# Two query chunks interleaved, a negation moved to VectorE, twelve more tiles on VectorE, three more warm products

## The chip, the cores and the metric

One Trainium2 chip, one core. The time is device microseconds of one execution of the whole program; lower is better. Engine names in the profile: PE is TensorE (PEld its weight loads), ACT is ScalarE, DVE is VectorE, POOL is GpSimd, SP is SyncE, whose queue issues most DMAs.

## The reference

Two attention blocks read the same `x` (2048 tokens, 512 wide, 32 heads of 16) and are mixed by a gate per token:

```python
g = sigmoid((x * gate_w).sum(-1, keepdims=True))
# a: softmax attention
scores = einsum("bhqd,bhkd->bhqk", q, k) * Dh ** -0.5
a = einsum("bhqk,bhkd->bhqd", softmax(scores), v) @ A_wo
# b: linear attention with softmax features
pq, pk = q @ w_phi[h], k @ w_phi[h]
phi_q = concat([softmax(pq), softmax(-pq)])       # phi_k likewise from pk
kv, z = einsum("bhsf,bhsd->bhfd", phi_k, v), phi_k.sum(s)
b = ((phi_q @ kv) / (phi_q @ z + 1e-6)) @ B_wo
out = g * a + (1 - g) * b
```

Branch A has 32 x 2048 x 2048 exponentials, which is by far the largest piece of elementwise work. Branch B has the features, their sums, and a small matrix per head.

## The kernel before

**Branch A.** The queries are cut into 4 chunks (`qc`) of 512, the heads into 4 pairs of groups (`cp`, 128 columns, each with two sides). A *group* is one chunk, one `cp` and one side: four heads of it lie in the four strips of 32 rows of the PE array. There are 32 groups. Each group runs over 16 key tiles of 128 tokens; a key tile of a group is a *row* of the schedule, numbered `p` from 0 to 511, and consists of 4 *units* of 128 keys x 512 queries, one per head. So a group is 64 units, and the kernel has 2048. Each unit is a score product (`_scores`, L1015, into PSUM), an exponential, and a value product (`_values`, L1122) that adds into the group's accumulator, one PSUM bank. Groups follow each other in the order chunk, `cp`, side: first all of chunk 0, then all of chunk 1, and so on.

**Two engines take the exponentials.** Most units go through ScalarE, two at a time (`_exp`, L1063, 128x1024 from a ring of four PSUM banks into `ET`). The rest, `NUMS[g]` of the 64 in group `g`, go to VectorE in batches of four (`_vector_batch`): VectorE writes the bits of an approximate power of two (L922, one 128x512 instruction per unit, from PSUM), and two more instructions per batch (L947, 2048 and 4096 elements) make three shifted copies. All four copies go through value products, two of them with the scaled values `V2`, so a unit on VectorE costs four value products where a unit on ScalarE costs one. `NUMS` adds up to 488 units (x488 at L922).

**Feeding it.** `_proj_k` (evacuated at L770), `_proj_v` (L819) and `_proj_q` (L783, then a mask on GpSimd at L788) make the keys, values and queries of a `cp` shortly before its rows. `_proj_q0`/`_proj_k0` do the first 512 tokens in two halves of 256, since `x` arrives in pieces by transposing DMAs; nine products on constant data (`_warm`, L689) run on PE before that. After a group, `_norm` transposes the accumulator (L1143), and after both sides it scales by reciprocal row sums and the gate, and sends the result back through DMAs on the SP queue into `onTA`.

**Branch B** is work for the gaps of the same engines. `_b_pair` handles two token tiles: two products with their evacuations (L1281), the negated copy (`b_neg`, L1299, GpSimd), maxima (L1302, L1304), a subtraction (L1307), one exponential on ScalarE (L1310), sums and reciprocals, the last mostly on GpSimd (L1314 to L1373), and a product (L1357). All of this is a chain on one buffer. Keys come first (8 pairs, due from row 30 on, every 23 rows, with `_b_v`, L1258, and `_b_kv`, L1400), then queries (8 pairs, due from row 214 on, every 30.5 rows, followed by `_b_den` and `_b_num`, L1451 to L1475). `_gate` computes the gate and copies it (`ghB`, L862, four small copies named `gate_b`). `_out` adds both output projections in PSUM and writes the tile out (L1599); in the last chunk alternate tiles go over ScalarE (L1596).

**The order is planned when the program is built.** `Plan.order` simulates the five engines with a table of costs and puts every operation into a fixed queue per engine; at run time each engine goes through its queue and waits on semaphores. Operations carry a due row (`prio`), an earliest row (`rel`) and a row from which they go ahead of everything (`urgent`). Names in `PORT` may not overlap GpSimd's work in the plan. `SEEDS` shifts the due rows by pseudo-random amounts, so that another set of numbers gives another order throughout. Where PE would idle, the plan puts in products with zeros (L1129, "fills"), which keep the array at work; `PADK` is the number of the first ScalarE score group that may be padded so in the start. Four PSUM banks are the ring of ScalarE, the other four are shared by accumulators, VectorE's scores and all projections.

Of the kernel before, what the change touches and what calls it, by code (L numbers as in the profile page):

```python
# [10 lines left out]
P = 128  # L11
# [54 lines left out]
class Plan:  # L66
# [70 lines left out]
        self.ops.append(o)  # L137
        return o

    SEEDS = (6713, 8236, 795, 8928, 4203, 3987, 4548, 4431, 3369, 6855, 1992, 9096, 3816, 673, 8476, 4153, 2488, 5053, 9892, 380, 9864, 6961, 8928, 7398, 8610, 6258, 6732, 8778, 7190, 2318, 6568, 0, 527, 0)  # L140

    def shift(self):
        count = {}
# [30 lines left out]
    SAME = 100  # L174
    OPEN = 2
    HURRY, FREE = 20, 30
    PORT = ("v_step", "b_neg", "b_max", "b_sub", "b_sum", "b_total", "b_mul", "n_mul", "n_den", "kvbd")
    HOLDING = ("kproj", "qproj", "bv", "pq", "vproj", "outa", "outb", "wtr", "xtr")

    def rank(self, o):  # L180
# [227 lines left out]
class _Kernel:  # L408
# [8 lines left out]
    KEEP = 15  # L417
    URGENT, AHEAD, SOON, REST = 4, -(1 << 30), 4, 6
    QDUE, KDUE, VDUE = 20, 17, 14
    P_Q, P_MUL, P_NEG = 1, 1, 1  # L420
    P_REC, P_SUM = 0, 4
    P_BACK, RATIO, BV = 1, 1, 8
    DEN, KV2, P_MAX = 1, 0, 0
    REND = 5
    P_M, P_BMUL, CHUNKS = 0, 0, 2
    GDUE = 26
    VMIN = 8
    FAST = 3
    VSOON = -2
    PADK = 8  # L430
    LAST, FIRST_OUT, NEXT_OUT, DEP_OUT = 0, 8, 0, 2
    ALONE, EARLY = 12, 10
    PVP = 10
# [1 line left out]
    def __init__(self, nc, A_x, A_wqkv, A_wo, B_wqkv, B_w_phi, B_wo, gate_w, out):  # L435
        self.nc = nc
        self.x2d = A_x.flatten_outer_dims()
        self.A_wqkv, self.A_wo = A_wqkv, A_wo
        self.B_wqkv, self.B_w_phi, self.B_wo = B_wqkv, B_w_phi, B_wo
        self.gate_w, self.out2d = gate_w, out.flatten_outer_dims()  # L440
        self.S = self.x2d.shape[0]
        self.NT = self.S // TOK
        self.NQC = self.S // QCH
        self.NPACK = self.NQC * 8 * self.NT
        self.plan = Plan()

    def build(self):
        with ExitStack() as ctx:
# [233 lines left out]
        job.bank = bank  # L682
        return job, (job if bank is None else None)

    def _warm(self, n, after):

        def run(e):
            for _ in range(n):
                ins = e.matmul(self.ps[:, 4, :], self.warm[:, 0:P], self.warm[:], start=True, stop=True)  # L689
            return ins  # L690
        self.plan.op("PE", run, 0.427 * n, reads=[self.b_warm], deps=[after], name="warm", prio=-99)

    COLS = 0

# [44 lines left out]
    def _proj_q0(self, half, bank):  # L739

        lo, op, ends = 256 * half, self.plan.op, []
        job, pool = self._job(bank)
        m = None
        for c in range(4):
            m = op("PE", lambda e, c=c: e.matmul(self._bank(job)[:, 0:256], self.WA[:, 0, c, 0:P],
                                                 self.xT[:, c, lo:lo + 256], start=(c == 0), stop=(c == 3)),
                   self.c_pe(256), reads=[self.b_x0[half], self.b_WA[0][0]], deps=[m], name="qproj", prio=half - 2.2,
                   acquire=None if c else pool)
            m.urgent = half - 99
        for side in range(2):  # L750
            dst, by = self.qT[:, side, lo:lo + 256], self.mask[:, side:side + 1]
            if half or side:
                o = op("DVE", lambda e, dst=dst, by=by: e.tensor_scalar(dst, self._bank(job)[:, 0:256], by, None,
                                                                        op0=ALU.mult), self.c_dve(256) + 0.06,
                       deps=[m] + ends, reads=[self.b_mask], name="q0_ev", prio=side - 2, release=pool if side else None)
            else:
                o = op("ACT", lambda e, dst=dst, by=by: e.activation(dst, self._bank(job)[:, 0:256], ACT.Copy, scale=by),
                       self.c_act(256) + 0.1, deps=[m], reads=[self.b_mask], name="q0_ev", prio=-2)
            self.b_qT[side].writers.append(o)
            if side == 0:  # L760
                self.b_q0[half].writers.append(o)
            ends.append(o)
        self.early.setdefault(bank, []).extend(ends)

    def _proj_k(self, cp, j):
        due = 32 * cp + 3 * j - self.KDUE if cp else 4 * j - 2.0
        self._proj(lambda c: self.WA[:, 1, c, P * cp:P * cp + P],
                   lambda c: self.xT[:, c, QCH * j:QCH * j + QCH],
                   [self.b_xT[j], self.b_WA[1][cp > 0]],
                   [lambda e, b: e.tensor_copy(self.kT[:, cp, QCH * j:QCH * j + QCH], b)],  # L770
                   self.c_dve(512), due, due - (24 if cp else 99), "kproj", [self.b_kT[cp][j]],
                   urgent=32 * cp + 4 * j - self.SOON)

    def _proj_q(self, qc, cp):
        n = qc * 4 + cp
        due = 32 * n - self.QDUE
        s0 = 2 * (n % (self.NQS // 2))

        lhs, rhs = lambda c: self.WA[:, 0, c, P * cp:P * cp + P], lambda c: self.xT[:, c, QCH * qc:QCH * qc + QCH]
        reads = [self.b_xT[qc], self.b_WA[0][cp > 0], self.b_mask]  # L780
        if self.P_Q:
            tmp, b_tmp = self.qtmp[:, n % 2, :], self.b_qtmp[n % 2]
            o = self._proj(lhs, rhs, reads, [lambda e, b: e.tensor_copy(tmp, b)], self.c_dve(512), due, 32 * n - 30, "qproj",  # L783
                           [b_tmp], urgent=32 * n - self.SOON)
            o.deps += [r for r in b_tmp.readers if r not in o.deps]
            b_tmp.readers = []
            for side in range(2):
                x = self.plan.op("POOL", lambda e, side=side: e.tensor_scalar(  # L788
                    self.qT[:, s0 + side, :], tmp, self.mask[:, side:side + 1], 0.0, op0=ALU.mult, op1=ALU.add), 0.7,
                    reads=[b_tmp, self.b_mask], writes=[self.b_qT[s0 + side]], name="qmask", prio=due + 1)  # L790
                x.urgent = o.urgent
            return
        self._proj(lhs, rhs, reads,
                   [lambda e, b: e.tensor_tensor(self.qT[:, s0:s0 + 2, :], b[:, None, :].to_broadcast([P, 2, QCH]),
                                                 self.mask[:, :, None].to_broadcast([P, 2, QCH]), ALU.mult)],
                   self.c_dve(1024), due, 32 * n - 30, "qproj", [self.b_qT[s0]], urgent=32 * n - self.SOON)
        self.b_qT[s0 + 1] = self.b_qT[s0]

    def _proj_v(self, pr, t0):

        op, NT = self.plan.op, self.NT
        job = Job()
        due = 64 * pr + t0 - (self.VDUE if pr else 0.5)
        mm = None
        for tt in range(2):
            def run(e, tt=tt):
                out = self._bank(job).rearrange("p (c t x) -> p c t x", c=2, t=2)[:, :, tt, :]
                for c in range(4):
# [2 lines left out]
                return ins  # L811
            mm = op("PE", run, 4 * self.c_pe(256), reads=[self.b_xT[t0 // 4], self.b_WA[2][pr]], deps=[mm], name="vproj",
                    prio=due, rel=due - 24 if pr else 0 if t0 < 4 else -99, acquire=None if tt else job)
            mm.urgent = 64 * pr + t0 - self.VSOON
        lo, n = t0 * self.VCP, 2 * self.VCP
        both = lambda v: v[:, 2 * pr * NT * self.VCP:(2 * pr + 2) * NT * self.VCP].rearrange(
            "p (c x) -> p c x", c=2)[:, :, lo:lo + n]
# [47 lines left out]
                prio=100))  # L865
        self.b_gB.writers = done

    NUMS = (6, 10, 12, 14, 14, 15, 13, 16, 13, 20, 17, 13, 16, 13, 19, 21, 10, 18, 12, 16, 19, 13, 17, 16, 15, 20, 12, 19, 17, 16, 23, 13)

    def _plan_vector(self):  # L870

        NT, away = self.NT, []
# [8 lines left out]
            self.hooks.setdefault(max(0, int(due) - 4), []).append(  # L881
                lambda k=k, units=units, due=due: self._vector_batch(k, units, due))
        for n in range(1, 4 * self.NQC):
            self.hooks.setdefault(max(0, 32 * n - 30), []).insert(0, lambda n=n: self._proj_q(*divmod(n, 4)))
        self.away = set(away)

    def _value_bufs(self, bufs, p, spill):

        kt, cp = p % self.NT, p // (2 * self.NT) % 4
        at = cp * self.NT + kt  # L890
        found = list(bufs[cp][kt // 2].writers)
        if spill and at + 1 < 4 * self.NT:
# [3 lines left out]
    def _vector_batch(self, number, units, due):  # L896
# [46 lines left out]
        for k in range(4):  # L943
# [9 lines left out]
            for g in sorted({u // (4 * NT) for u in units}):  # L953
# [3 lines left out]

                def run(e, g=g, src=src, ot=ot, v=v, tile=tile, place=place):
                    for j, u in src:
                        ins = self._values(e, ot, g % 8, u // 4 % NT, {u % 4: tile[:, place(j), :].bitcast(BF16)}, v)  # L960
                    return ins
                x = op("PE", run, 0.23, reads=[buf], deps=list(found.values()), name="pvx", prio=units[0] / 4 - 2,
                       kind="col", array=0.0533 * len(src), strips=[u % 4 for _, u in src])
# [5 lines left out]
    def _attention(self):  # L969
# [24 lines left out]
        while a < len(self.mine):  # L994
# [4 lines left out]
            done = self.mine[a] if a < len(self.mine) else NU  # L999
            while len(self.pvs) < done // 4:  # L1000
                self._pv(len(self.pvs))
                if len(self.pvs) % (8 * NT) == 0:
                    self._out(len(self.pvs) // (8 * NT) - 1)

    def _unit(self, u):

        p, i = divmod(u, 4)
        g, kt = divmod(p, self.NT)
        qc, g8 = divmod(g, 8)
        s = 2 * ((qc * 4 + g8 // 2) % (self.NQS // 2)) + g8 % 2  # L1010
        return p, i, kt, g8 // 2, s

    def _scores(self, e, u, out, cols=slice(0, QCH)):
# [56 lines left out]
    def _pv(self, p):  # L1070
# [13 lines left out]
        def run(e):  # L1084
            for _ in range(o.filled):
                self._fill(e, ot)
            return self._values(e, ot, g % 8, kt, src, self.V)
        o = self.plan.op("PE", run, 0.23, reads=[self.b_zero], deps=deps, name=f"pv{p}", prio=p + self.PVP, kind="col",
                         acquire=None if kt else ot, array=0.0533 * len(src), strips=list(src))
        plan = self.plan  # L1090
# [40 lines left out]
        return ins  # L1131

    def _norm_a(self, g, last):
        qc, g8 = divmod(g, 8)
        return self._norm(qc, lambda: self._bank(self.ot[g]), g8 % 2, last, self.onTA[:, qc % 3, g8 // 2, :],
                          self.b_onTA[qc % 3][g8 // 2], 16 * g + 17.0, self.ot[g], g >= self.NPACK // self.NT - 2)

# [430 lines left out]
    def _out(self, qc):  # L1568
        op, NT, NQC = self.plan.op, self.NT, self.NQC
        for tt in range(4):  # L1570
            t = 4 * qc + tt
            final = qc == NQC - 1
            due = max(128 * (qc + 1) + 8 + 4 * tt, self._num_due(t) + 8)
            job, first = self.outs[t]
            b_onTA = self.b_onTA[qc % 3]
            if final:
# [70 lines left out]
```

## Time and profile before

| | |
|---|---|
| three runs | 767.77 us median, 766.18 to 769.58 |
| the profiled execution | 767.62 us; span on the core 765.6 us |
| ScalarE busy | 749.1 us, 98% of the span |
| TensorE busy (modelled ends) | 739.6 us, 97% |
| VectorE busy | 711.6 us, 93% |
| GpSimd busy | 207.5 us, 27% |
| granted TensorE clock | 0.997 of full in the mean |

The profile's page gives busy time per engine, the span in 40 slices, the chain of waits that ended last, and groups of equal instructions with their busy time, the mean duration of one and the idle time before them. Instructions on one engine overlap a little: a mean duration is longer than busy time over count, and the distance of two starts is the better price. The span runs from the first to the last instruction; what lies around it is the 2.0 us between 765.6 and 767.62.

### The profile page before, as it was taken

What the parts mean: (1) busy time and instruction counts of PE and PEld (TensorE: products, weight loads), DVE (VectorE), ACT (ScalarE), POOL (GpSimd) and SP (SyncE); (2) the same over time, 40 slices, a digit from 0 to 9 for tenths busy, and PEclk for the clock granted to TensorE, in tenths of its full rate; (3) what the DMA queues carried; (4) which work ended last, traced back from release to release, by engine and by line L of the source; (5) the groups of instructions that cost most, each with busy time, mean ns of one, the idle gap of its engine ahead of it and who ended that gap; (6) DMA issues with size and microseconds to landing.
All of it is one profiled execution on the core that took longest, in us unless ns stands there. A gap on an engine that the chain in (4) does not pass through costs nothing.

```text
span 765.6 us, 17042 instructions
## 1 busy us (share of the span) xinstructions
PE 739.6 (97%) x7149; PEld 219.6 (29%) x7220; DVE 711.6 (93%) x1110; ACT 749.1 (98%) x804; POOL 207.5 (27%) x301
## 2 busy tenths in 40 slices
PE   8999999999999999999999999999999999999998
PEld 3322233222222222222332322232222222222222
DVE  4778997899999999999999999999999999999995
ACT  6999999999999999999999999999999999999996
POOL 2210255315053260405145023422314140250000
PEclk9999999999999999999999999999999999999999
DMA  9501001000000000010121202211111121011000
GB/s 232 127 2 28 3 14 15 1 2 8 9 3 14 1 3 14 1 15 2 15 29 28 53 11 51 45 27 30 32 26 28 29 47 24 15 30 27 5 12 28
DMA packets 89180, 20.78 MB, mean 27 GB/s; under 512 B 83472, under 2 KB 88592, under 8 KB 89104
## 3 DMA queue, kind: packets, MB, share of 16 engines
q1 hardware_dynamic: 87232, 18.92, 13.4%
q8 instruction: 56, 0.92, 0.5%
q10 hardware_dynamic: 1872, 0.79, 0.4%
q14 instruction: 20, 0.16, 0.1%
HBM read 4.21 MB, written 2.10 MB: 8 GB/s over the span
## 4 chain that ended last, share of the span: by engine, by line
ACT 76%; PE 15%; DVE 9%; issue 1%
ACT ET L1063 73%; PE ps L1015 5%; PE ps L1122 5%; PE ps L698 3%; ACT bq L1310 3%; DVE vs L922 3%; DVE vs L947 2%; PE ps L1129 1%; PE ps L689 1%; DVE onB L1475 1%; DVE T L1143 0%; DVE bq L1307 0%; DVE btree L1304 0%; DVE ghB L862 0%; DVE qtmp L783 0%
## 5 line engine op out<-in xcount | busy, mean ns | idle before, releaser
L1063 ACT ACTIVATE ET<-ps 128x1024 bf16<-128x1024 f32 (+1 forms) x782 | 720.4, 1154 | 3.7 <-PE ps L1015 3.6
L922 DVE TENSOR_SCALAR vs<-ps 128x512 uint16<-128x512 f32 x488 | 313.7, 679 | 20.7 <-PE ps L1015 19.7
L1015 PE MATMUL ps<-qT,kT 32*128 32x512 bf16 (+1 forms) x2052 | 312.4, 385 | 13.1 <-ACT ET L1063 8.0
L947 DVE TENSOR_SCALAR vs<-vs 128x2048 uint16<-128x2048 uint16 (+1 forms) x244 | 235.4, 977 | 1.9 <-PE ps L1122 0.5
L1122 PE MATMUL ps<-vs,V 128*32 128x512 bf16 x1952 | 216.4, 384 | 1.4 <-DVE vs L947 1.4
L1122 PE MATMUL ps<-ET,V 128*32 128x512 bf16 x1560 | 194.5, 387 | 0.1
L1015 PEld LDWEIGHTS ps<-qT,kT 32*128 32x128 bf16 x2052 | 78.0, 91 | 309.3 <-ACT ET L1063 293.2
L1314 POOL TENSOR_TENSOR btree<-btree 128x512 f16<-128x512 f16 (+1 forms) x32 | 33.4, 1044 | 188.8 <-DVE btree L1312 188.0
L1122 PEld LDWEIGHTS ps<-ET,V 128*32 128x32 bf16 x1560 | 48.9, 94 | 84.1 <-issue 75.8
L1129 PE MATMUL ps<-kT,zero 128*32 128x512 bf16 x628 | 63.4, 385 | 0.0
L1122 PEld LDWEIGHTS ps<-vs,V 128*32 128x32 bf16 x1952 | 49.8, 95 | 45.9 <-issue 27.5
L1299 POOL TENSOR_SCALAR bq<-bq 128x1024 bf16<-128x1024 bf16 x16 | 21.5, 1341 | 150.6 <-DVE bq L1281 119.5
L698 PE MATMUL ps<-WB,xT 128*128 128x512 bf16 x160 | 49.6, 383 | 2.8 <-issue 2.1
L1160 POOL TENSOR_TENSOR T<-T,rinv 128x512 bf16<-128x512 f32 x15 | 18.2, 1210 | 83.4 <-DVE rinv L1158 83.2
L698 PE MATMUL ps<-xT,WA 128*128 128x512 bf16 x101 | 33.2, 392 | 1.9 <-issue 1.6
L788 POOL TENSOR_SCALAR qT<-qtmp,mask 128x512 bf16<-128x512 bf16 x30 | 25.8, 866 | 28.8 <-DVE qtmp L783 28.5
L1143 DVE STREAM_TRANSPOSE T<-ps 128x512 f32<-128x512 f32 x32 | 22.6, 707 | 11.2 <-PE ps L1122 11.1
L1310 ACT ACTIVATE bq<-bq 128x2048 bf16<-128x2048 bf16 x16 | 32.1, 2007 | 0.2
L1281 DVE CAST bq<-ps 128x512 bf16<-128x512 f32 x32 | 21.7, 680 | 0.3 <-PE ps L698 0.2
L826 POOL TENSOR_SCALAR V<-V 128x544 bf16<-128x544 bf16 x16 | 12.6, 788 | 33.4 <-DVE V L819 33.2
L698 PEld LDWEIGHTS ps<-WB,xT 128*128 128x128 bf16 x192 | 13.3, 97 | 25.3 <-issue 20.5
L1129 PEld LDWEIGHTS ps<-kT,zero 128*32 128x32 bf16 x628 | 14.7, 94 | 19.7 <-issue 18.8
(88 smaller groups left out, 405.3 us busy)
## 6 DMA issues: line engine op xcount, KB each, us to landing
T<-T SPq DMA_DIRECT2D x240, 8.0 KB, 1.8
WB<-in_B_wqkv_dram SPq DMA_DIRECT2D x1, 1536.0 KB, 7.9
out_dram<-WB SPq DMA_DIRECT2D x12, 128.0 KB, 1.7
WA<-in_A_wqkv_dram SPq DMA_DIRECT2D x2, 384.0 KB, 5.4
WoB<-in_B_wo_dram SPq DMA_DIRECT2D x1, 512.0 KB, 3.8
WoA<-in_A_wo_dram SPq DMA_DIRECT2D x1, 512.0 KB, 4.8
WA<-in_A_wqkv_dram ACTq DMA_DIRECT2D x2, 128.0 KB, 3.1
WA<-in_A_wqkv_dram ACTq DMA_DIRECT2D x1, 256.0 KB, 4.6
```

Of the source, the lines that this page charges most:

```text
L698: return e.matmul(out, lhs, rhs, start=start, stop=stop)
L788: x = self.plan.op("POOL", lambda e, side=side: e.tensor_scalar(self.qT[:, s0 + side, :], tmp, self.mask[:, side:side + 1], 0.0, op0=ALU.m ...
L922: bits = lambda e, to, src: e.tensor_scalar(to, src, SCALE * LOG2E * 128.0, float(ORIGIN), op0=ALU.mult, op1=ALU.add)
L947: o = op("DVE", lambda e, k=k, src=src, dst=dst: e.tensor_scalar(dst, src, float(STEPS[k - 1]), None, op0=ALU.add), 0.16 + k * n * QCH * 0 ...
L1015: return e.matmul(out[:, cols], self.kT[32 * i:32 * i + 32, cp, kt * TOK:(kt + 1) * TOK], self.qT[32 * i:32 * i + 32, s, cols], start=True ...
L1063: o = plan.op("ACT", lambda e: e.activation(self.ET[:, a % NS:a % NS + n, cols], self.ps[:, a % NR:a % NR + n, cols], ACT.Exp, scale=SCALE ...
L1122: ins = e.matmul(self._bank(ot)[32 * i:32 * i + 32, :], v[:, v0:v0 + 32], tile, start=(kt == 0), stop=(kt == self.NT - 1), tile_position=( ...
L1129: ins = e.matmul(self._bank(ot)[32 * i:32 * i + 32, :], self.zero[:], self.kT[:, 0, 0:QCH], start=False, stop=False, tile_position=(0, 32 ...
L1143: t1 = op("DVE", lambda e: e.transpose(T1[:, side].rearrange("p b s -> p (b s)"), src()), 0.735, deps=last, writes=[b_T1[side]], name="n_t ...
L1281: [lambda e, b, k=k: e.tensor_copy(bq[:, k].rearrange("p (g s v) -> p g s v", g=8, s=2)[:, :, 0, :], b.rearrange("p (g v) -> p g v", g=8))],
L1310: op("ACT", lambda e: e.activation(flat, flat, ACT.Exp), 1.789, reads=[b], writes=[b], name="b_exp", prio=due + 1)
L1314: + [("b_sum", two(128 * n), lambda e, n=n: e.tensor_tensor(half[:, :, 0:n], half[:, :, 0:n], half[:, :, n:2 * n], ALU.add), (n <= self.P_ ...
```

## The change

1. **Order of the groups.** With `PAIRQ = 1`, `self.pairs` lists chunk 0 and chunk 1 alternately for each `cp`: (0, cp 0), (1, cp 0), (0, cp 1), (1, cp 1) and so on to row 256; chunks 2 and 3 follow as before. `use[cp]` is the first row of a `cp`, now 0, 64, 128, 192 in place of 0, 32, 64, 96. The due rows of `_proj_k`, `_proj_q` and `_proj_v` follow it; for the second half of the values `use` is 128 plus the tile, but row 95 for the first two tiles. Chunk 0 is complete at row 224 in place of 128 (`done`), which is when its output may be due.
2. **Warm products.** Three more products on constant data, into bank 1, after the first half of the first query projection (`WARM = 3`).
3. **`P_NEG = 0`**: the 16 `b_neg` go from GpSimd to VectorE.
4. **`NUMS`**: 500 units on VectorE in place of 488. By eight groups: 111, 127, 127, 135 in place of 100, 132, 121, 135.
5. **Plan**: new `SEEDS`, `gate_b` and `gwb` added to `PORT`, `PADK` 2 in place of 8.

```diff
-    SEEDS = (6713, 8236, 795, 8928, 4203, 3987, 4548, 4431, 3369, 6855, 1992, 9096, 3816, 673, 8476, 4153, 2488, 5053, 9892, 380, 9864, 6961, 8928, 7398, 8610, 6258, 6732, 8778, 7190, 2318, 6568, 0, 527, 0)
+    SEEDS = (5206, 4574, 4516, 849, 7476, 2999, 2928, 1228, 1442, 3304, 7242, 2072, 255, 3792, 7272, 0, 9567, 6248, 9008, 9950, 2895, 6157, 2030, 1780, 7230, 8440, 1271, 7931, 6690, 9122, 5090, 0, 4360, 0)
...
-    PORT = ("v_step", "b_neg", "b_max", "b_sub", "b_sum", "b_total", "b_mul", "n_mul", "n_den", "kvbd")
+    PORT = ("v_step", "b_neg", "b_max", "b_sub", "b_sum", "b_total", "b_mul", "n_mul", "n_den", "kvbd", "gate_b", "gwb")
...
-    P_Q, P_MUL, P_NEG = 1, 1, 1
+    P_Q, P_MUL, P_NEG = 1, 1, 0
...
+    PAIRQ = 1
...
-    PADK = 8
+    PADK = 2
...
+        pairs = [(qc, cp) for cp in range(4) for qc in range(2)] if self.PAIRQ else [(qc, cp) for qc in range(2) for cp in range(4)]
+        self.pairs = pairs + [(qc, cp) for qc in range(2, self.NQC) for cp in range(4)]
+        self.seq = [(qc, 2 * cp + side) for qc, cp in self.pairs for side in range(2)]
+        self.use = [32 * next(n for n, x in enumerate(self.pairs) if x[1] == cp) for cp in range(4)]
+        self.done = [32 * max(n + 1 for n, x in enumerate(self.pairs) if x[0] == qc) for qc in range(self.NQC)]
...
+        if self.WARM and not half:
+            self.early.setdefault(1, []).append(self._warm(self.WARM, m, bank=1, cost=0.215, prio=-2.15))
...
-        due = 32 * cp + 3 * j - self.KDUE if cp else 4 * j - 2.0
+        due = self.use[cp] + 3 * j - self.KDUE if cp else 4 * j - 2.0
...
-        due = 64 * pr + t0 - (self.VDUE if pr else 0.5)
+        use = self.use[2 * pr] + t0
+        if pr and not t0:
+            use = min(use, self.use[1] + 31)
+        due = use - (self.VDUE if pr else 0.5)
...
-    NUMS = (6, 10, 12, 14, 14, 15, 13, 16, 13, 20, 17, 13, 16, 13, 19, 21, 10, 18, 12, 16, 19, 13, 17, 16, 15, 20, 12, 19, 17, 16, 23, 13)
+    NUMS = (6, 10, 16, 14, 14, 16, 16, 19, 13, 19, 17, 12, 17, 11, 19, 19, 14, 20, 12, 16, 19, 13, 17, 16, 15, 20, 12, 20, 17, 16, 22, 13)
...
-        kt, cp = p % self.NT, p // (2 * self.NT) % 4
+        kt, cp = p % self.NT, self.pairs[p // (2 * self.NT)][1]
...
-        qc, g8 = divmod(g, 8)
-        s = 2 * ((qc * 4 + g8 // 2) % (self.NQS // 2)) + g8 % 2
+        g8 = self.seq[g][1]
+        s = 2 * (g // 2 % (self.NQS // 2)) + g8 % 2
...
-            due = max(128 * (qc + 1) + 8 + 4 * tt, self._num_due(t) + 8)
+            due = max(self.done[qc] + 8 + 4 * tt, self._num_due(t) + 8)
```

More of the change, by code (lines that the diff above doesn't have):

```diff
@@ L683, in _job, with _warm @@
         return job, (job if bank is None else None)
-    def _warm(self, n, after):
+    def _warm(self, n, after, bank=4, cost=0.427, prio=-99):
         def run(e):
             for _ in range(n):
-                ins = e.matmul(self.ps[:, 4, :], self.warm[:, 0:P], self.warm[:], start=True, stop=True)
+                ins = e.matmul(self.ps[:, bank, :], self.warm[:, 0:P], self.warm[:], start=True, stop=True)
             return ins
-        self.plan.op("PE", run, 0.427 * n, reads=[self.b_warm], deps=[after], name="warm", prio=-99)
+        return self.plan.op("PE", run, cost * n, reads=[self.b_warm], deps=[after], name="warm", prio=prio)
+    WARM = 3
     COLS = 0
@@ L771, in _proj_k, with _proj_q @@
                    self.c_dve(512), due, due - (24 if cp else 99), "kproj", [self.b_kT[cp][j]],
-                   urgent=32 * cp + 4 * j - self.SOON)
-    def _proj_q(self, qc, cp):
-        n = qc * 4 + cp
+                   urgent=self.use[cp] + 4 * j - self.SOON)
+    def _proj_q(self, n):
+        qc, cp = self.pairs[n]
         due = 32 * n - self.QDUE
@@ L813, in _proj_v @@
                     prio=due, rel=due - 24 if pr else 0 if t0 < 4 else -99, acquire=None if tt else job)
-            mm.urgent = 64 * pr + t0 - self.VSOON
+            mm.urgent = use - self.VSOON
         lo, n = t0 * self.VCP, 2 * self.VCP
@@ L883, in _plan_vector @@
         for n in range(1, 4 * self.NQC):
-            self.hooks.setdefault(max(0, 32 * n - 30), []).insert(0, lambda n=n: self._proj_q(*divmod(n, 4)))
+            self.hooks.setdefault(max(0, 32 * n - 30), []).insert(0, lambda n=n: self._proj_q(n))
         self.away = set(away)
     def _value_bufs(self, bufs, p, spill):
-        kt, cp = p % self.NT, p // (2 * self.NT) % 4
+        kt, cp = p % self.NT, self.pairs[p // (2 * self.NT)][1]
         at = cp * self.NT + kt
@@ L959, in run @@
                     for j, u in src:
-                        ins = self._values(e, ot, g % 8, u // 4 % NT, {u % 4: tile[:, place(j), :].bitcast(BF16)}, v)
+                        ins = self._values(e, ot, self.seq[g][1], u // 4 % NT, {u % 4: tile[:, place(j), :].bitcast(BF16)}, v)
                     return ins
@@ L1001, in _attention @@
                 self._pv(len(self.pvs))
-                if len(self.pvs) % (8 * NT) == 0:
-                    self._out(len(self.pvs) // (8 * NT) - 1)
+                if len(self.pvs) in self.done:
+                    self._out(self.done.index(len(self.pvs)))
     def _unit(self, u):
@@ L1086, in run @@
                 self._fill(e, ot)
-            return self._values(e, ot, g % 8, kt, src, self.V)
+            return self._values(e, ot, self.seq[g][1], kt, src, self.V)
         o = self.plan.op("PE", run, 0.23, reads=[self.b_zero], deps=deps, name=f"pv{p}", prio=p + self.PVP, kind="col",
@@ L1133, in _norm_a @@
     def _norm_a(self, g, last):
-        qc, g8 = divmod(g, 8)
+        qc, g8 = self.seq[g]
         return self._norm(qc, lambda: self._bank(self.ot[g]), g8 % 2, last, self.onTA[:, qc % 3, g8 // 2, :],
```

## The prediction

> **What bounds the kernel now.** I read the page first, for the engines and the chain of waits, then the groups by shape, then busy time by stretches.
>
> ```profile
> span 765.6 us, 17042 instructions
> ...
> PE 739.6 (97%) x7149; PEld 219.6 (29%) x7220; DVE 711.6 (93%) x1110; ACT 749.1 (98%) x804; POOL 207.5 (27%) x301
> ...
> DVE  4778997899999999999999999999999999999995
> ACT  6999999999999999999999999999999999999996
> ...
> ACT 76%; PE 15%; DVE 9%; issue 1%
> ```
> ```profile
> L1063 ACT ACTIVATE ET<-ps 128x1024 bf16<-128x1024 f32 x778 | 718.3, 1157 | 3.3 <-PE ps L1015 3.2
> ...
> L1299 POOL TENSOR_SCALAR bq<-bq 128x1024 bf16<-128x1024 bf16 x16 | 21.5, 1341 | 150.6 <-DVE bq L1281 119.5 <-DVE VB L1258 26.4 <-DVE bq L1357 4.6
> ...
> L1302 DVE TENSOR_TENSOR btree<-bq 128x1024 bf16<-128x1024 bf16 x16 | 10.8, 676 | 1.3 <-POOL bq L1299 1.3
> ```
>
> ScalarE carries 76% of the chain, and its 778 full exponentials waited only 3.3 us in all. Outside the start and the tail it is never free. One exponential of two tiles costs 718.3 / 778 = 0.923 us of its time; the 1157 ns include the overlap with the next. VectorE looks free by its average (93%), but the row of slices says where: in the first eight. The next view gives this in microseconds.
>
> ```profile
> core 0: us, PE busy (x) PEld busy (x) DVE busy (x) ACT busy (x) POOL busy (x), PEclk, DMA share, GB/s
> 0.00:20.00 20.00, 17.75 (x94) 6.64 (x96) 9.67 (x19) 12.64 (x16) 5.62 (x17) 0.91 1.00 237
> 20.00:160.00 140.00, 136.40 (x1168) 43.32 (x1180) 117.80 (x181) 138.61 (x151) 35.74 (x51) 1.00 0.12 24
> 160.00:750.00 590.00, 573.28 (x5799) 165.68 (x5852) 577.08 (x901) 589.05 (x629) 166.12 (x233) 1.00 0.12 21
> ```
> ```profile
> 200.00:600.00 400.00, 389.04 (x3883) 113.11 (x3917) 392.33 (x616) 399.15 (x425) 126.32 (x181) 1.00 0.12 21
> 500.00:600.00 100.00, 97.12 (x999) 27.84 (x1004) 98.76 (x156) 99.83 (x108) 27.05 (x36) 1.00 0.14 26
> 160.00:205.00 45.00, 43.53 (x424) 12.82 (x432) 44.61 (x73) 45.00 (x49) 13.79 (x18) 1.00 0.05 7
> ```
>
> VectorE idles 22.2 us between 20 and 160 us (16%), but only 12.9 us in the 590 us after (2.2%). Two engines are full from 160 us on. What counts is whether work can move from ScalarE into VectorE's early gap.
>
> **The change, part by part.**
>
> *Twelve more tiles on VectorE.* ScalarE loses 12 tiles, six exponentials: 6 x 0.923 = **-5.5 us** on the path. VectorE's price is read from distances of starts:
>
> ```profile
> 98.35 1.21 DVE L947 TENSOR_SCALAR vs<-vs 128x4096 uint16<-128x4096 uint16 x1
> 99.48 1.87 DVE L922 TENSOR_SCALAR vs<-ps 128x512 uint16<-128x512 f32 x3
> ...
> 104.00 0.68 DVE L1281 CAST bq<-ps 128x512 bf16<-128x512 f32 x1
> 104.60 0.68 DVE L947 TENSOR_SCALAR vs<-vs 128x2048 uint16<-128x2048 uint16 x1
> 105.20 0.68 DVE L922 TENSOR_SCALAR vs<-ps 128x512 uint16<-128x512 f32 x1
> ```
>
> The 4096 step takes 1.13 us, the 2048 step and a 128x512 piece 0.60 each. A tile is 0.60 plus a quarter of 1.73, that is 1.03 us; twelve are 12.4 us. Eleven of them land in the first eight groups (111 for 100), where the gap is; groups 16 and 17 get six more, groups 8 to 15 give five up. On TensorE each tile has three more value products:
>
> ```profile
> L1122 PE MATMUL ps<-vs,V 128*32 128x512 bf16 x1952 | 216.4, 384 | 1.4 <-DVE vs L947 1.4
> L1122 PE MATMUL ps<-ET,V 128*32 128x512 bf16 x1560 | 194.5, 387 | 0.1
> L1129 PE MATMUL ps<-kT,zero 128*32 128x512 bf16 x628 | 63.4, 385 | 0.0
> ```
>
> That is 48 x 0.111 - 12 x 0.125 = 3.8 us, and the 63.4 us of zero products that fill PE's holes cover it. If the holes lie elsewhere, 3.8 us is the cost.
>
> *The negation.* POOL loses 21.5 us that is off the path; VectorE's maxima waited 1.3 us in all for it. VectorE gains 16 two-byte operations of 1024 elements. Nearest row: L947, the same instruction, 0.60 us for 2048 and 1.13 for 4096, so 0.53 per 2048 and 0.34 for 1024: 5.4 us in all, the value I take. The other end is the pace of a 128x512 copy, 0.60 for 512 elements, with 0.53 more for the other 512: 1.13 each, 18.1 us.
>
> *VectorE's balance.* Between 20 and 750 us it works 117.80 + 577.08 = 694.9 us; now 694.9 + 12.4 + 5.4 = 712.7. ScalarE would need 730 - 5.5 - 1.4 (the stall below) = 723.1. That leaves 10.4 us, 1.4%, for VectorE's idle time. The best 100 us of the trace have 1.24% (cost 0), the 400 us from 200 to 600 have 1.92% (712.7 / 0.9808 = 726.7, cost 3.6), the whole from 160 to 750 has 2.19% (728.7, cost 5.6). Part of that idle time is only pacing by ScalarE and can close; I take the middle of the first two, **+1.8 us**, and keep 0 to 5.6.
>
> *Interleaving.* It removes no work; projections of keys for the second `cp` on move back by 32, 64 and 96 rows, and most of the second half of the values from about row 50-64 to 116-130. It should remove this stall:
>
> ```profile
> 89.92 2.01 DVE L862 COPY ghB<-gh 32x16 f32<-32x16 f32 x4
> ...
> 91.95 0.69 DVE L770 CAST kT<-ps 128x512 bf16<-128x512 f32 x1
> ...
> 92.70 0.38 PE L1015 MATMUL ps<-qT,kT 32*128 32x512 bf16 x1 [1.28 <-DVE kT L770]
> ...
> 94.20 1.94 ACT L1063 ACTIVATE ET<-ps 128x1024 bf16<-128x1024 f32 x2 [1.39 <-PE ps L1015]
> ```
>
> VectorE reaches the evacuation of the keys only after four copies of the gate that took 2.01 us beside GpSimd's work; a score product behind it in PE's queue waits for the bank, and ScalarE idles 1.39 us. With the keys of the third `cp` due 64 rows later, and the copies planned apart from GpSimd, I count **-1.4 us**; the other end is 0, with another crowd there. Chunk 0's output is held back to row 224, which costs nothing: its first evacuation came only when branch B delivered, at 410 us:
>
> ```profile
> L1599 DVE CAST WB<-ps x12: 672/680/692, 410.1 to 636.5; 128x512 bf16<-128x512 f32 x12
> ...
> L819 DVE CAST V<-ps x16: 680/693/695, 15.1 to 140.2; 128x512 bf16<-128x512 f32 x16
> L770 DVE CAST kT<-ps x15: 672/680/694, 13.6 to 174.8; 128x512 bf16<-128x512 f32 x15
> ```
>
> The same normalisations, DMAs of SP's queue, masks on POOL and query projections remain, in another order; none is on the chain, so their move is counted at nothing. If a head pair's return through SP were late, only an output would wait, and outputs have the rows to 750 us.
>
> *Start: warm products and `PADK`.*
>
> ```profile
> 8.22 3.17 ACT L1063 ACTIVATE ET<-ps 128x512 bf16<-128x512 f32 x5 [0.47 <-PE ps L1015]
> 11.94 2.10 ACT L1063 ACTIVATE ET<-ps 128x1024 bf16<-128x1024 f32 x2 [0.55 <-PE ps L1015]
> 14.54 3.84 ACT L1063 ACTIVATE ET<-ps 128x1024 bf16<-128x1024 f32 x4 [0.50 <-PE ps L1015]
> ```
> ```profile
> 7.02:10.43 3.41, 2.76 (x21) 1.30 (x21) 2.00 (x4) 2.69 (x6) 0.00 (x0) 1.00 1.11 235
> 10.43:13.85 3.42, 3.42 (x13) 0.89 (x12) 1.46 (x4) 2.81 (x3) 0.00 (x0) 0.50 1.08 223
> ...
> 7.08 0.33 PEld L745 LDWEIGHTS ps<-xT,WA 128*128 128x128 bf16 x4 [0.38 <-DMA xT<-in_A_x_dram]
> ...
> L689 PE MATMUL ps<-warm 128*128 128x512 bf16 x9 | 4.0, 631 | 1.5 <-DVE warm L620 1.5
> ```
>
> The first exponential starts at 8.22. After a stretch in which PE was busy 2.76 of 3.41 us the granted clock was 0.50 for 3.4 us, and ScalarE waited 0.55 + 0.50 around it: at most -1.05 to gain. Three products at the pace of the nine (4.0 / 9 = 0.45 each) put 1.34 us ahead of the second half of `x`, of which 0.38 was a wait for the DMA anyway: at most +0.96 to lose. With the clock of 1.00 granted from 7.02 on they may take half of that, and the loss is 0.3. Half the gain and that loss give **-0.3 us** (rounded).
> The Trainium skill, "TensorE: Matmul & The Clock Gate", section "What's actually happening", ties the half clock to an idle window of about 3.4 us. By that rule a stretch with 2.76 us busy would not cost the clock, more products would gain nothing, and the sum would be 0.6 us higher; this trace, with 0.50 right after such a stretch, does not agree.
>
> *Sum:* -5.5 + 1.8 - 1.4 - 0.3 = -5.4 us. The profiled execution took 767.6 us for a span of 765.6, and lies 0.15 under the median; so 762.2, and I say **762 us**.
>
> **The rivals.**
>
> *VectorE becomes the bound.* For it: from 160 us on it idles only 2.2%, and groups 16 and 17 with their six new tiles lie where there is no room. Against: 22.2 us of early gap, and branch B's chains are free to move. With the three gains (5.5 + 1.4 + 0.3 = 7.2) and 2.19% idle: 767.6 - 7.2 + 5.6 = 766.0 us, no change. Should the negation cost 1.13 each, the work is 725.4, 734.5 us at 1.24% idle, 11.4 above 723.1: 772.
>
> *The postponed projections crowd rows 96 to 128* (the slower case). That is 160 to 205 us, where VectorE was busy 44.61 of 45. Added there: up to seven value evacuations (4.2), six tiles in groups 6 and 7 (6.2), two negations (0.7), while ScalarE needs 2.8 less: 13.9, less 0.4 idle, 13.5 us. The keys cost nothing, since others stood there before (until 174.8 us). If none of it moves, 767.6 - 7.2 + 13.5 = 774 us. Slower by over 0.5% only if under 2.3 of the 13.5 moves away; branch B's two pairs in that stretch can wait, so I think most does.
>
> *The stall moves instead of going, and the start gains nothing:* 767.6 - 5.5 + 1.8 = 763.9 us, on the border of the 0.5% (3.8 us) that a measurement can tell from no change.
>
> *VectorE gets time back from GpSimd.*
>
> ```profile
> L947 DVE TENSOR_SCALAR vs<-vs x244: 622/1163/1949, 18.2 to 752.2; 128x2048 uint16<-128x2048 uint16 x113, 128x4096 uint16<-128x4096 uint16 x9
> ```
>
> Some L947 take 1.95 us where a 4096 step starts the next after 1.13: something holds them up. If the 21.5 us of negation on POOL were a part of it, VectorE's cost of 1.8 goes to 0: 760.4 us.
> The Trainium skill, "SBUF — State Buffer", section "SBUF: two separate sides", says that GpSimd and VectorE's two-port operations lock each other out for a whole instruction; the 1.95 us row agrees.
>
> **How the numbers follow.** The forecast (759 to 764) gets 0.57, time back from GpSimd 0.08, a stall that moves 0.07 (half on each side of the border), VectorE as bound at about 766 0.14, with the dear negation 0.03, the crowd 0.11. Faster: 0.57 + 0.08 + 0.03 = 0.68. Same: 0.04 + 0.14 = 0.18. Slower: 0.03 + 0.11 = 0.14. The range: everything at its best is 767.6 - 5.5 - 1.4 - 1.05 = 759.7, and 1 or 2 us less with the tail or ScalarE's last small waits (589.05 of 590): 758. Up: past the bound at 766 to where the dear negation and a half-absorbed crowd begin, 771. The forecast alone: 759 to 764.
>
> **What the profile after would show.** Six full exponentials fewer at L1063 with the same 0.92 us each; VectorE between 20 and 160 us at 93% or more, and 98.5% later; L1299 on DVE at 0.34 to 0.45 us; no idle time of ScalarE over 1 us near 93 us; full clock from 10.4 to 13.9 us. I would be wrong if ScalarE waits for TensorE by more than some 5 us in all between 20 and 750 us, above all from 160 to 205 or around groups 16 and 17.

## The result and the profile after

| | before | after |
|---|---|---|
| median of four runs each | 768.43 us | 759.44 us (759.41 to 760.18) |
| ratio | | 0.9892, 95% interval 0.9869 to 0.9915 |
| profiled execution, span | 767.62, 765.6 | 759.47, 757.7 |

1.1% faster; 762 was forecast, with 759 to 764 for the likeliest case. From profile to profile the time fell by 8.15 us where the forecast's sum was 5.4. Part of the 9.0 us between the medians hangs on the clock, which both profiles of the old start lose there (last section): the kernel before varies with its mean granted clock, 766.1 to 766.7 us in the eight of 39 runs beside the experiments in which it was 0.999 or 1.000, some 767.7 at 0.997, 770.3 to 770.8 at 0.993, while the changed kernel's four runs all show 0.999 or 1.000. At full clock the gain is nearer 7 us.

From the page of the changed kernel, first busy time and slices, then the chain:

```profile
span 757.7 us, 17122 instructions
...
PE 747.0 (99%) x7215; PEld 218.8 (29%) x7215; DVE 721.0 (95%) x1144; ACT 742.7 (98%) x798; POOL 188.6 (25%) x285
...
DVE  4779999999999999999999999999999999999995
ACT  6999999999999999999999999999999999999995
...
ACT 75%; PE 15%; DVE 9%; DMA 1%; issue 0%; DVEq 0%
```

VectorE's gap in the first eight slices has closed from the fourth slice on. Groups by shape of the changed kernel (its L1076 is the exponential of L1063 before, L935 is L922, L1312 the negation):

```profile
L1076 ACT ACTIVATE ET<-ps 128x1024 bf16<-128x1024 f32 x772 | 712.4, 1164 | 1.0 <-PE ps L1028 0.8
L935 DVE TENSOR_SCALAR vs<-ps 128x512 uint16<-128x512 f32 x500 | 322.5, 684 | 10.9 <-PE ps L1028 9.2
...
L960 DVE TENSOR_SCALAR vs<-vs 128x4096 uint16<-128x4096 uint16 x125 | 153.9, 1234 | 0.8 <-PE ps L1135 0.5
...
L1312 DVE TENSOR_SCALAR bq<-bq 128x1024 bf16<-128x1024 bf16 x16 | 6.7, 419 | 0.1
...
L875 DVE COPY ghB<-gh 32x16 f32<-32x16 f32 x4 | 1.1, 267 | 0.1
```

Six exponentials fewer (712.4 us for 718.3), and ScalarE was idle 1.0 us before them where it had been 3.3. Busy time by stretches, changed kernel (columns as in the prediction's view):

```profile
0.00:20.00 20.00, 17.62 (x105) 6.88 (x105) 10.51 (x20) 13.09 (x17) 5.61 (x17) 1.00 1.00 225
20.00:160.00 140.00, 139.04 (x1235) 42.05 (x1233) 129.56 (x207) 139.72 (x151) 35.79 (x56) 1.00 0.13 26
160.00:750.00 590.00, 585.72 (x5859) 167.95 (x5858) 577.37 (x914) 588.86 (x630) 147.16 (x212) 1.00 0.13 21
...
160.00:205.00 45.00, 45.00 (x432) 13.52 (x430) 43.51 (x69) 45.00 (x49) 12.80 (x19) 1.00 0.07 8
```

From 20 to 160 us VectorE works 129.56 us for 117.80, and ScalarE idles 0.28 us for 1.39. The span fell by 7.9 us: ScalarE's busy time by 6.4 (749.1 to 742.7), its idle time by 1.5, of which 1.1 lie between 20 and 160 us and 0.45 in the first 20 us (13.09 busy for 12.64); the rest cancels. Two of the prediction's signs were missed: VectorE was to be busy 93% or more of 20 to 160 us and 98.5% later, and shows 92.5% and 97.9%.

### The profile page after: what moved, and what is told of

It is laid out like the page before. It is cut to its first block, busy times and chain, and to the rows that moved or that the text cites. A ratio compares the mean times of both kernels' runs of the same rounds, so it can differ in the third digit from the quotient of the medians.

```text
span 757.7 us, 17122 instructions
## 1 busy us (share of the span) xinstructions
PE 747.0 (99%) x7215; PEld 218.8 (29%) x7215; DVE 721.0 (95%) x1144; ACT 742.7 (98%) x798; POOL 188.6 (25%) x285
## 4 chain that ended last, share of the span: by engine, by line
ACT 75%; PE 15%; DVE 9%; DMA 1%; issue 0%; DVEq 0%
ACT ET L1076 72%; PE ps L1028 5%; PE ps L1135 5%; ACT bq L1323 4%; DVE vs L935 3%; DVE vs L960 3%; PE ps L706 2%; PE ps L822 1%; DMA xT<-in_A_x_dram 1%; PE ps L1142 1%; DVE kT L780 0%; DVE bq L1320 0%; PE ps L1254 0%; DVE bq L1294 0%; DVE btree L1317 0%; DVE T L1156 0%
## 5 line engine op out<-in xcount | busy, mean ns | idle before, releaser
L1076 ACT ACTIVATE ET<-ps 128x1024 bf16<-128x1024 f32 (+1 forms) x776 | 714.6, 1161 | 1.6 <-PE ps L1028 1.5
L935 DVE TENSOR_SCALAR vs<-ps 128x512 uint16<-128x512 f32 x500 | 322.5, 684 | 10.9 <-PE ps L1028 9.2
L960 DVE TENSOR_SCALAR vs<-vs 128x2048 uint16<-128x2048 uint16 (+1 forms) x250 | 239.3, 971 | 1.1 <-PE ps L1135 0.5
L1135 PE MATMUL ps<-vs,V 128*32 128x512 bf16 x2000 | 210.9, 384 | 0.6 <-DVE vs L935 0.4
L1135 PE MATMUL ps<-ET,V 128*32 128x512 bf16 x1548 | 192.6, 387 | 0.8 <-DVE vs L935 0.8
L1135 PEld LDWEIGHTS ps<-ET,V 128*32 128x32 bf16 x1548 | 48.7, 94 | 80.6 <-issue 70.8
L1135 PEld LDWEIGHTS ps<-vs,V 128*32 128x32 bf16 x2000 | 48.6, 95 | 52.1 <-issue 32.4
L1142 PE MATMUL ps<-kT,zero 128*32 128x512 bf16 x584 | 59.8, 385 | 0.0
L706 PE MATMUL ps<-WB,xT 128*128 128x512 bf16 x192 | 59.6, 384 | 0.0
L798 POOL TENSOR_SCALAR qT<-qtmp,mask 128x512 bf16<-128x512 bf16 x30 | 22.8, 767 | 83.1 <-DVE qtmp L793 82.9
L706 PE MATMUL ps<-xT,WA 128*128 128x512 bf16 x120 | 38.1, 384 | 0.0
L1320 DVE TENSOR_TENSOR bq<-bq,btree 128x2048 bf16<-128x2048 bf16 x16 | 19.6, 1223 | 0.1
```

Source lines behind the costliest of these rows:

```text
L706: return e.matmul(out, lhs, rhs, start=start, stop=stop)
L935: bits = lambda e, to, src: e.tensor_scalar(to, src, SCALE * LOG2E * 128.0, float(ORIGIN), op0=ALU.mult, op1=ALU.add)
L960: o = op("DVE", lambda e, k=k, src=src, dst=dst: e.tensor_scalar(dst, src, float(STEPS[k - 1]), None, op0=ALU.add), 0.16 + k * n * QCH * 0 ...
L1076: o = plan.op("ACT", lambda e: e.activation(self.ET[:, a % NS:a % NS + n, cols], self.ps[:, a % NR:a % NR + n, cols], ACT.Exp, scale=SCALE ...
L1135: ins = e.matmul(self._bank(ot)[32 * i:32 * i + 32, :], v[:, v0:v0 + 32], tile, start=(kt == 0), stop=(kt == self.NT - 1), tile_position=( ...
L1142: ins = e.matmul(self._bank(ot)[32 * i:32 * i + 32, :], self.zero[:], self.kT[:, 0, 0:QCH], start=False, stop=False, tile_position=(0, 32 ...
```

## The experiments

The theory after the result: the twelve tiles shorten ScalarE's list, and the interleaving gives VectorE something to do early, so that the tiles fit. Rivals: the start, GpSimd's silence, fewer waits alone, or simply a luckier order out of the new seeds.

### The warm products, order unchanged (e1)

```diff
-                ins = e.matmul(self.ps[:, bank, :], self.warm[:, 0:P], self.warm[:], start=True, stop=True)
+                w = QCH if bank == 4 else 1
+                ins = e.matmul(self.ps[:, bank, 0:w], self.warm[:, 0:P], self.warm[:, 0:w], start=True, stop=True)
```

> The changed kernel, order of every queue unchanged, with the three new warm products cut to one column each, so that they take almost no time. If they keep the clock at 1.00 from 10.4 to 13.9 us and that is worth what the prediction counted, the granted clock falls to 0.50 there again and the time rises by 0.5 to 1.0 us (760 to 760.5). If the half clock does not depend on them, the clock stays and the time falls by up to 0.7 us, since the second half of x is projected earlier.

Measured: 759.24 us, the time of the changed kernel (759.44). In the profiled execution the clock stays, as in the second expectation, and next to nothing is gained. Three of the four runs took 758.99 to 759.47 us at a mean clock of 1.000; the fourth took 761.19 at 0.998. Busy time in the two stretches of the start, e1:

```profile
7.02:10.43 3.41, 2.74 (x18) 0.99 (x18) 2.14 (x4) 2.61 (x5) 0.00 (x0) 1.00 1.15 220
10.43:13.85 3.42, 3.33 (x22) 1.39 (x21) 1.81 (x3) 2.84 (x3) 0.00 (x0) 1.00 1.07 224
```

PE was busy 2.74 us of the first stretch, no more than before (2.76), and yet the granted clock of the second is 1.00. So full clock does not need the warm products, and in three runs of four their loss cost nothing. Whether they make the loss of the clock rarer is open: the fourth run lost some, none of the changed kernel's four did, and where it lost it is not on record. What else in the new start keeps the clock was not separated; the order may, or the fills that `PADK = 2` allows (the profile shows two at 9.75 us; the kernel before has its first at 392 us).

### One part undone, everything planned anew (e2, e3, e4), and nothing undone (e8)

```diff
e2   -    P_Q, P_MUL, P_NEG = 1, 1, 0
     +    P_Q, P_MUL, P_NEG = 1, 1, 1
e3   -    PAIRQ = 1
     +    PAIRQ = 0
e4   -    NUMS = (6, 10, 16, 14, 14, 16, 16, 19, ... )
     +    NUMS = (6, 10, 12, 14, 14, 15, 13, 16, ... )   # all 32 as before, 488
e8   -    SEEDS = (5206, 4574, 4516, 849, ... )
     +    SEEDS = (0,) * 34
```

> The changed kernel with the negation planned on GpSimd again. If the 5.4 us on VectorE were near its limit, as the prediction's balance has it, the time falls by 0 to 2 us (757.5 to 759.5). If VectorE gained time by GpSimd's silence, it rises by 1 to 3 us (760.5 to 762.5) and the long L947 become more. A rise beyond that would be the changed order, not the negation.

> The changed kernel with the old order of the groups (chunk by chunk), 500 tiles kept. If the interleaving is what makes room for the eleven early tiles, ScalarE waits again in the first 160 us, by 3 to 8 us in all (762 to 768). If the room was there anyway, only the stall of 1.4 us comes back (760 to 761).

> The changed kernel with the old 488 tiles. If ScalarE's list sets the time, six exponentials more cost 6 x 0.92 = 5.5 us (765). If the gain came from fewer waits and not from the list, it stays within 2 us of 759.4.

> The changed kernel with all seeds zero: due rows as written, nothing shifted. The three re-planned kernels came out 33 to 40 us slower than the changed one. If that was their undone parts, this one, which undoes none, stays within 5 us of 759. If it was that the seeds no longer fit the plan, it is 20 to 40 us slower too (780 to 800).

Measured: 795.2, 799.2 and 794.0 us, and 784.2 for e8 with no part undone. All theories were off for the first three, by some 30 us, and e8 says why: the change with all its parts, but without seeds made for it, is 24.7 us slower than with them and 2% slower than the kernel before. So e2 to e4 measure mostly the loss of a fitted order, and nothing on the parts can be read from them. Where it goes, e8, waits of ScalarE (in total, times, longest):

```profile
ACT ET L1076 <- PE ps L1135: 15.9, 4, 6.5
ACT xT L1609 <- PE ps L706: 12.2, 2, 11.9
```

Exponentials wait for value products (L1135), which must free a slot of `ET` first, four times for up to 6.5 us; and at the end the last output waits 11.9 us for its projection where it waits 4.0 in the changed kernel. Whether the kernel before without its seeds is as slow was not run.

### The negation, order of all else unchanged (e5, e6)

After planning, the 16 operations are taken out of one queue and put into the other at their planned start.

```diff
+        for o in [o for o in self.queues["DVE"] if o.name == "b_neg"]:
+            self.queues["DVE"].remove(o)
+            at = sum(x.start < o.start for x in self.queues["POOL"])
+            self.queues["POOL"].insert(at, o)
+            o.eng = "POOL"
```

(e5, on the changed kernel; e6 is the same on the kernel before, with DVE and POOL exchanged.)

> The changed kernel with every queue as it is, only the 16 negations taken out of VectorE's queue and put into GpSimd's at the place of their planned start. If the negation on VectorE fills time that was idle anyway, taking its 6.7 us (16 x 0.42) away gains at most 1 us, and GpSimd's 1.1 to 2 us per negation, now ahead of the maxima in branch B's chain, make VectorE wait: 760 to 770, as that chain's lateness reaches tiles queued behind it on VectorE. If VectorE were the bound, the time would fall by up to 5 us.

> The kernel before with every queue as it is, only the 16 negations taken out of GpSimd's queue and put into VectorE's. The prediction's balance: 5.4 us more on an engine with 2.2% idle, in the worst case 5.4 us slower (773 to 774). If VectorE's true slack is larger than its busy share shows, or GpSimd's silence gives time back: within 1.5 us of before.

Measured: e5 761.86 us, 2.4 more than the changed kernel. e6 768.49 us beside 767.71 for before, ratio 1.0011 (0.9994 to 1.0028). Groups of e5:

```profile
L1317 POOL TENSOR_SCALAR bq<-bq 128x1024 bf16<-128x1024 bf16 x16 | 22.6, 1415 | 73.9 <-DVE bq L1299 39.5 <-DVE VB L1276 32.2 <-DVE bq L1375 2.2
...
L1320 DVE TENSOR_TENSOR btree<-bq 128x1024 bf16<-128x1024 bf16 x16 | 10.8, 677 | 2.1 <-POOL bq L1317 2.1
```

and e5's busy time:

```profile
PE 736.1 (97%) x7145; PEld 219.4 (29%) x7215; DVE 718.6 (95%) x1128; ACT 743.4 (98%) x798; POOL 211.4 (28%) x301
```

VectorE lost 6.7 us of work, but its busy time fell only from 721.0 to 718.6 and its idle time rose from 36.7 to 41.5 (span 760.1). Part of what it saved it spent waiting, 2.1 us directly for the negation. Of the 2.4 us, 0.4 lie in the first 20 us (ScalarE busy 12.69 for 13.09), before the first negation at 76.8 us, so they are not its doing; that leaves about 2.

In the kernel before, 16 more instructions on VectorE cost little: the interval of the ratio holds 1. Among runs of equal granted clock e6 is 0.7 to 0.9 us slower (at 0.998, a middle of 768.4 us for 767.6), so most of the 6.7 us found room there, not quite all.

### VectorE's slack (e7)

```diff
-               ("b_max", two(1024), lambda e: e.tensor_tensor(tree, x[:, :, 0:8], x[:, :, 8:16], ALU.max),
+               ("b_max", two(1024), lambda e: [e.tensor_tensor(t, x[:, :, 0:8], x[:, :, 8:16], ALU.max) for t in (
+                tree, self.scratch[:].rearrange("p (n f i) -> p n f i", n=32, f=8))][-1],
```

> The changed kernel, queues unchanged, with the first maximum of each pair done a second time into a spare tile: 16 more VectorE instructions of 0.60 us, 9.6 us. By busy time VectorE has 34 us idle in all, some 17 between 20 and 750 us. If it has real slack there, the time rises by under 3 us; if VectorE is as much the bound as ScalarE, by 6 to 10 us (765 to 769).

Measured: 767.15 us, 7.7 more for 9.6 us of work (16 times 0.60). In the profiled execution 0.8 us of that were lost in the first 20 us (ScalarE busy 12.30 for 13.09), before the first maximum at 80.9 us, so the work itself cost about 7. Between 20 and 750 us, first the changed kernel, then e7:

```profile
20.00:750.00 730.00, 724.76 (x7092) 210.00 (x7091) 706.93 (x1119) 728.58 (x780) 182.95 (x268) 1.00 0.13 22
```
```profile
20.00:750.00 730.00, 709.27 (x6961) 210.62 (x7025) 712.51 (x1128) 726.01 (x774) 183.07 (x268) 1.00 0.12 21
```

In the changed kernel VectorE idles 23.1 us of these 730, and yet little of it took up new work. ScalarE does the same 798 instructions, but over the whole span its busy time rose by 3.8 us (742.7 to 746.5) and its idle time by 4.3: VectorE holds it up. VectorE is now nearly as much the bound as ScalarE.

### One part undone, order fitted again (e9 to e12)

To compare parts, each variant needs an order of its own quality. The seeds of each were fitted in the same way: for every stretch of 16 rows some 24 to 30 random values, those kept with which the plan is ahead by its own table of costs; three fits of each variant (four of e12), the best by that table taken. Fits of one variant differ, so the differences are less certain than the intervals of the runs.

```diff
e9    SEEDS (8670, 3349, 4486, ...)                 all parts of the change
e10   SEEDS (0, 3549, 2118, ...)     P_NEG = 1      negation on GpSimd
e11   SEEDS (0, 9096, 3615, ...)     NUMS as before 488 tiles
e12   SEEDS (4244, 3187, 9786, ...)  PAIRQ = 0      chunk by chunk
```

> The changed kernel with seeds newly fitted to its plan, as in the next three: row segment by row segment, the set kept that ends earliest by the plan's table of costs. This one undoes nothing and is what the next three are compared with. If fitted order is what the level of 759 rests on, another fitted set gives it too: 757 to 761. If the original seeds hold something that such a fit does not find, 765 or more.

> Negation planned on GpSimd, seeds fitted anew. e2 was 36 us slower with seeds made for another plan. If that was the seeds and not the negation, this comes to within 2 us of e9 (757 to 762). If VectorE needs the negation for its chain, 763 or more.

> 488 tiles, seeds fitted anew. If ScalarE's list sets the time: six exponentials of 0.92 us more than e9, 5.5 us (763 to 765.5). If VectorE is the tighter of the two, its 12.4 us less give part of that back: within 3 us of e9.

> Chunk by chunk again, 500 tiles, negation on VectorE, seeds fitted anew. If the interleaving makes the room for the tiles, no order is as good without it: 766 to 775, with ScalarE's waits between 20 and 400 us. If its worth was only the stall of 1.4 us near 93 us: 759 to 762.

| | median us | to e9 | ratio to before |
|---|---|---|---|
| e9, all parts | 758.47 (758.14 to 758.72) | | 0.9879 (0.9857 to 0.9901) |
| e10, negation on GpSimd | 761.51 | +3.0 | 0.9923 (0.9901 to 0.9945) |
| e11, 488 tiles | 763.35 | +4.9 | 0.9943 (0.9922 to 0.9963) |
| e12, chunk by chunk | 771.33 | +12.9 | 1.0046 (1.0029 to 1.0063) |

e9 is the fastest kernel here; its runs all lie below those of the changed kernel, by 1.0 us in the median, though the two were not run side by side and their ratios' intervals overlap.

The 3.0 us of e10 can't be read as the price of the negation's place, for two thirds of them lie at one spot. One stretch of e9, then of e10:

```profile
390.00:580.00 190.00, 185.60 (x1861) 54.30 (x1879) 187.36 (x304) 190.00 (x204) 48.07 (x70) 1.00 0.19 33
```
```profile
390.00:580.00 190.00, 183.93 (x1869) 53.44 (x1880) 185.72 (x292) 188.02 (x202) 52.58 (x69) 0.99 0.17 30
```

ScalarE idles 1.98 us in this stretch of e10, and 0.00 in e9. PE waits up to 1.65 us, until 519.73, for a transposing DMA of the query features (`phiT`) that took 5.1 us to land where the median is 3.3, and then the granted clock is 0.50 from 520.46 to 523.88. All six runs of e10 have a mean clock of 0.996 to 0.998. Whether the move made that DMA late is not shown; e8, with the negation on VectorE, has a half clock at 520.73 too.

Busy time of e9 and of e11:

```profile
PE 733.8 (97%) x7115; PEld 218.0 (29%) x7187; DVE 719.5 (95%) x1144; ACT 742.9 (98%) x798; POOL 187.2 (25%) x285
```
```profile
PE 737.3 (97%) x7136; PEld 218.1 (29%) x7201; DVE 711.6 (93%) x1126; ACT 747.9 (98%) x804; POOL 188.0 (25%) x285
```

Without the tiles ScalarE works 5.0 us longer and the span is 4.9 longer (761.6 for 756.7): the list sets the time. Without the interleaving the tiles did not fit in any order that was found. Stretches of e9, then of e12:

```profile
20.00:160.00 140.00, 137.03 (x1230) 42.46 (x1244) 128.29 (x206) 139.98 (x152) 38.25 (x56) 1.00 0.12 25
```
```profile
20.00:160.00 140.00, 136.78 (x1210) 43.28 (x1225) 121.82 (x191) 138.80 (x152) 27.25 (x36) 1.00 0.12 26
```

Chunk by chunk, VectorE gets 6.5 us less done between 20 and 160 us, GpSimd 11.0 us less. That work must be done later. Where e12's time goes, its waits of ScalarE show:

```profile
ACT xT L1609 <- PE ps L706: 11.4, 1, 11.4
ACT ET L1076 <- PE ps L1135: 3.5, 2, 2.3
ACT ET L1076 <- PE ps L1028: 3.1, 6, 1.3
```

and its chain of waits after the last exponential, which ends at 754.5 us:

```profile
755.11 6.02 PE ps L706 x27
761.13 1.66 PE ps L1135 x28
```

Of the 13.1 us between the spans (769.8 and 756.7), 7.6 are the end: the last output waits 11.4 us for 3.8 in e9. In e9 20 projections stand last on PE (4.44 us); in e12 27 do, and the last group's value products and its normalisation come only behind them. On the way ScalarE's exponentials waited 6.6 us for 1.7 in e9. That the early work left undone is what lengthens the end was not tested: the kernel before, chunk by chunk with 488 tiles, has an end of 3.8 us, so a better set of seeds might shorten e12's.

## Why the prediction was right or wrong

**Twelve tiles, -5.5: right.** Their group lost 5.9 us in the profile, and fitting without them costs 4.9 (e11).

**VectorE's balance, +1.8: the step that failed, in size and in kind.** In size: its cost was 0, since from 160 to 740 us ScalarE idled 0.07 us in all. The three groups that grew gained 8.8 + 4.5 + 6.7 = 20.0 us of busy time, near the 17.8 predicted, but the engine's busy time rose by 9.4 only. The difference is overlap. An instruction whose successor is already waiting overlaps with it by about 0.08 us (0.68 long, 0.60 apart); the durations of all VectorE's instructions add up to 785.7 us before and 809.0 after, 23.3 more, so the overlap grew by 14 us. In kind: idle time by busy share is not slack. The balance would have left e7 room for its 9.6 us in the 23.1; it cost 7.7.

**The negation, "off the path" on GpSimd and a cost on VectorE: wrong in sign.** Its price was right: it is 0.42 us long, and where other work is waiting the next instruction starts 0.33 us after it; 0.34 was taken. But in the changed kernel it is worth about 2 us to have it on VectorE (e5); e10 can't confirm this, since its loss lies mostly elsewhere. GpSimd has idle time enough, but branch B's chain passes through it, where the negation takes 1.04 us or more, and VectorE's fixed queue waits behind that chain, for 2.1 us in e5. The rival "time back from GpSimd" had the right sign, though not for its reason: the long L947 are hardly shorter (4096 elements: 1241 to 1234 ns; 155.0 us in all in e5 for 153.9).

**Interleaving, -1.4: right on the stall, far too small.** The stall is gone: ScalarE idles 0.28 us from 20 to 160, and the four copies take 1.1 us for 1.9. But the prediction counted only the stall and took the early gap as given room. The best order found without the interleaving gives 771.3 us with the same 500 tiles (e12), so the gap became room only with it; apart from its end, e12's exponentials alone waited 4.9 us longer. The forecast's "it removes no work" left out that work done early is not left for later; how much of e12's loss that is, and how much its seeds, is open.

**The start, -0.3: 0.45 by the trace, for a reason that stays open.** (Half of 1.05 less 0.3 is 0.2; the sum took 0.3.) The clock is at 1.00 and ScalarE's first 20 us hold 0.45 more work, but in e1's profile both come without the warm products. The term also took one profile for the kernel: by the runs at full clock the half clock costs the kernel before nothing in some runs, about 1.4 us in the middle and over 4 in others, as far as clock and time go together.

**Chunk 0's output and the moved steps at nothing: right.** No wait of ScalarE in the changed kernel is for them.

**The crowd at rows 96 to 128: did not come.** From 160 to 205 us ScalarE is busy 45.00 of 45, VectorE 43.51.

**What the prediction left out: the order.** It treated new seeds as neutral. Setting them to zero costs 24.7 us (e8 against the changed kernel), about three times the gain. The forecast held because the seeds fitted the change, which nothing in it weighed: that part was luck. With seeds of zero it would have been the slower case, with an exponential waiting for a slot of `ET` (L1135), a wait that no rival named.

## What to carry to other kernels

Where two engines are full and each has a fixed queue, an engine's idle share is not what it can still take: add a known dummy piece with the order unchanged (e7) before trusting a budget made from busy time. Early idle time on one engine pays only if work can be brought forward into it, and the other end of the program is to be looked at too (e12's tail). A part of a change that goes through a planner or scheduler can be priced only with the order fitted again for each variant, or with the queues held as they are; undone and planned anew it measures the planner.

## What was not expected of the hardware

The clock at the start. Both profiles with the old start lose it: before from 10.43 to 13.85 us, e6 from 11.66 to 18.49, twice as long. From e6, two stretches:

```profile
10.43:13.85 3.42, 3.33 (x16) 1.03 (x16) 1.96 (x4) 3.03 (x4) 0.00 (x0) 0.68 1.12 223
...
0.00:20.00 20.00, 16.58 (x76) 6.22 (x77) 8.30 (x17) 11.07 (x14) 5.62 (x17) 0.83 0.98 222
```

ScalarE gets 11.07 us of work done in e6's first 20 us, 12.64 in the kernel before, whose order is the same up to there. This, and not the negation, is most of the 2.5 us between these two executions, and it fits the spread of the kernel's other runs.

Nor does the share of recorded PE work in the stretch ahead decide it. In the kernel before, the half clock follows 3.41 us with 2.76 us of PE work; later in the same execution, from 88.94 us, 3.41 us hold only 2.46 and the clock stays at 1.00. What does decide it is open.

The Trainium skill, "TensorE: Matmul & The Clock Gate", section "What's actually happening", names an idle window of about 3.4 us as what brings the half clock. The kernel before does not agree, with 2.76 of 3.41 us busy just ahead of it; neither does e10, where PE's longest wait ahead of the half clock was 1.65 us.
